# Block-sparse attention into soft MoE: late weight pieces beside the last products, in quarters of rows, and combine turns and identity products in the last chain

## The chip, the cores and the metric

One core of a Trainium2 chip runs the whole program. The metric is the device time of one execution in microseconds, the median of several runs. Five engines work side by side: PE (TensorE, matrix products), DVE (VectorE), ACT (ScalarE), POOL (GpSimd), and SP (SyncE), which here only issues transfers. The transfers run on 16 engines that all queues share.

## The reference, cut to what matters

```python
def _attn_ref(q, k, v, sampled_blocks):          # 4 batches, 8 heads, 768 tokens, head size 64
    scores = scale * np.matmul(q, k.transpose(0, 1, 3, 2))
    # blocks of 32: a query block sees its neighbours, the first and the last block, and three
    # sampled blocks; the first and the last query block see everything
    ...
    attn = softmax(np.where(mask, scores, -1e9))
    return np.matmul(attn, v)

def _moe_ref(x, phi, w1, w2):                    # x: 3072 tokens of 512, phi: 512 x 32 slots
    logits = x @ phi
    d = softmax over the tokens;  slot_input = d.T @ x      # 8 experts, 4 slots each
    slot_out[e] = np.maximum(slot_input[e] @ w1[e], 0.0) @ w2[e]   # 512 -> 1024 -> 512
    c = softmax over the slots;   return c @ slot_out
```

All numbers are float32. [...]

## The kernel before, in words

**Attention.** A unit is two query blocks of one batch, all eight heads. POOL and ACT gather its 256 keys per block into a staging tile `kst` (L414 to L422) and its sampled V blocks into `vrs` (L438). PE makes the scores `s` (L493), DVE the row maximum (L508), ACT the exponential `p` (L513), DVE the turned `ptt` (L520), and PE the products with V, `av` (L571): blocks near the query and the first and last block come straight from the V buffer of the batch (`v0` or `v1`, by turns), sampled ones from `vrs`. DVE divides into `x` (L565 to L567). The first and the last query block are a dense unit (`sd`, `pd`, `ptd`, `avd`).

**First half of the MoE.** Four tiles of `x` make a group. PE turns them (`mxt`, L749), makes logits `ml`, and after an exponential the sums over tokens `ms` (L817). The last group's chain runs from the last `av` over `mxt`, `ml`, `lt`, `mr`, `md`, `ms`, `mc` to `psS` (L996), the slots, and then the first layer can start.

**What sets the order.** `Plan` holds all of this as tasks with a duration for an engine, and a key. `Plan.run` simulates the engines and writes the order out. Weight loads in it are paced: a piece hangs on the PE product that the plan has behind it at 0.22 MB per us.

**The weights** are 64 pieces of 1024 columns x 128 rows (0.5 MB). Two make a first-layer step (`pf`, L1103, pieces 0 to 31) or a second-layer step (`pso`, L1111, pieces 32 to 63). 11 pieces have a place of their own (`wpre`); pieces 11 to 25 go, during the last batch, into buffers that the attention no longer needs: `ktile` (`kw`), `v0`, `ptd`, and the last `ktile`. All these are loaded by quarters: four transfers of 32 rows. Then come nine *places* over the staging tiles (`Place`, 0 to 3 over `kst`, 4 over the scaled q, 5 to 8 over `vrs`), six pieces in `v1`, and after that whatever a step has freed (`done_w`). Of the places, the first five are loaded by quarters, the others, `v1` and all later pieces whole. The transfers of SP's queue use eight semaphores by turns, so that at most eight are under way.

**Second half.** The combine weights `c` of a token are split into two exact parts (`c_head` on DVE, L886, `c_rest` on POOL, L892) and turned by PE (`pc`, L906), one group of four token tiles after the other, between the first steps of the first layer. The output is `po` (L1209), evacuated into `ob` and stored from SP's queue (L1166 to L1174), in two halves of the columns; both halves' stores stand behind all weights in that queue.

```python
    NEND = len(wpool) + (NKST * NP * 256 + NQ * NP * 2 * BLK) // WP
    next_w([Place(n) for n in range(NLB)])
    load_group(LATEW[1])
```

Of the kernel before, what the change touches and what calls it, by code (L numbers as in the profile page):

```python
# [28 lines left out]
D1 = D + 1  # L29
NBZ = NB + 1  # L30
# [21 lines left out]
KW = {"ktile": 3, "v0": 6, "v1": 6, "ptd": 3}  # L52
H1, HALF = 3, 4
# [15 lines left out]
class Plan:  # L69
# [11 lines left out]
    def run(self):  # L81
# [69 lines left out]
        todo = {e: [t for t in order if t.eng == e and t.pre] for e in at}  # L151
        pe = []
# [17 lines left out]
def attn_moe_kernel(ctx, tc, qT, kT, vfull, vtab, sampled, phi, w1, w2, out):  # L170
# [32 lines left out]
    def new_wk(tag):  # L203
        k = KW[tag]
        if tag == "ktile":
            wk[tag] = pk.tile([P, k, WP], F32, name="kw", tag=tag)
        else:
            buf = ptdb if tag == "ptd" else vbuf[int(tag[1])]
            wk[tag] = buf[:, 0:k * WP].rearrange("p (k f) -> p k f", k=k)

    def load_wk(m, tag, j, rows=slice(0, P)):

        return load_w(m + j, None, wk[tag][:, j, :], rows)
# [33 lines left out]
    def index_math():  # L247
# [19 lines left out]
        DVE.tensor_tensor(out=vreg, in0=own, in1=tmp, op=ALU.add)  # L267
# [12 lines left out]
    vrs = [pst.tile([P, 2, NR, 2 * D1], F32, name=f"vrs{n}") for n in range(NVR)]  # L280
# [68 lines left out]
    def warm(t):  # L349

        st = psA.tile([P, 2, 256], F32, tag="s", name="st", bufs=SB)
        for j in range(12):
# [121 lines left out]
    def plan_pair(b, g, n):  # L474
# [21 lines left out]
        t_qk = add(qk, ("PE", 1.1), [t_q] + [k for _, k in kd], n, acq=[("s", s_use[0]), ("s", s_use[1])])  # L496
# [7 lines left out]
        for r in range(2):  # L504
# [18 lines left out]
            t_m = add(top, ("DVE", 0.59), [t_qk], n + 0.1 + 0.01 * r)  # L523
# [55 lines left out]
    def av_heads(T, rs_):  # L579
# [4 lines left out]
        for n, c in enumerate((4, 5)):  # L584
            for r in rs_:
                for g, s_ in G2:
                    av_mm(T.av, 64 * r if one else 0, m, g, r, T.pt[r][s_, c, 0:m // BLK].rearrange("p j q -> p (j q)"),
                          vt[s_, :, (0, NB - 1)[n], r, :], n == 0, False)
        for c in (1, 2):
            for w, u in enumerate(us):  # L590
                for r in rs_:
                    for g, s_ in G2:
                        av_mm(T.av, 64 * r if one else 64 * w, 64, g, r,
                              T.pt[r][s_, c, 2 * w:2 * w + 2].rearrange("p j q -> p (j q)"),
                              vt[s_, :, 2 * u.g + c, r, :], False, False)
        for n in range(NR + 1):
            for w, u in enumerate(us):
                for r in rs_:
                    for j in range(2):
                        i = 2 * u.g + 1 + j  # L600
                        for g, s_ in G2:
                            if n == 0:
# [4 lines left out]
                                v_ = vt[s_, :, k, r, :]  # L607
# [6 lines left out]
    def plan_av(T, n):  # L614
        deps = T.turned + T.staged + [t_v[T.b]]
        use, x_use = [], T.x_use
        if len(T.units) == 1:
# [7 lines left out]
            t_a = add(both, ("PE", 2.5), deps, n + 0.5, acq=[("av", use)])  # L625
            T.out = [add(out, ("DVE", 1.4), [t_a], n + 0.6)]
        else:
# [4 lines left out]
            t_0 = add(lambda t: heads(t, 0), ("PE", 2.2), deps, n + 0.5, acq=[("av", use)])  # L632
            t_a = add(lambda t: heads(t, 1), ("PE", 2.2), [t_0], n + 0.5)
            T.out = [add(lambda t: av_out(T, T.av, 0, P), ("DVE", 1.0), [t_a], n + 0.6, acq=[("x", x_use)])]
        x_use.extend(T.out)
        use.extend(T.out)
        v_use[T.b].append(t_a)
        for u in T.use + list(T.pt_use.values()):
# [5 lines left out]
    def plan_dense(b, j, n):  # L644
# [19 lines left out]
        t_q0, s_acq, s_cost = None, [("s", s_use[0])] * 2 + [("s", s_use[1])] * 2, 1.5  # L664
# [10 lines left out]
        for r in range(2):  # L675
# [24 lines left out]
            t_m = add(top, ("DVE", 0.56 if t_h else 1.12), [t_qk] + t_h, n + 0.1 + 0.01 * r)  # L700
# [7 lines left out]
        if j:  # L708
            use = []

            def dense(t):
                vt = vtile[b]
                T.avd = psA.tile([P, 2, 512], F32, tag="av", name="avd", bufs=1)
                for k in range(NB):
                    for r in range(2):
                        for g, s_ in G2:
                            av_mm(T.avd, 64 - 64 * r, 64, g, r, ptd[r][s_, k].rearrange("p j q -> p (j q)"), vt[s_, :, k, r, :],
# [9 lines left out]
            t_o = add(out, ("DVE", 1.4), [t_a] + T.out, n + 0.6)  # L727
# [14 lines left out]
    def plan_group(gi, Ts, last, final=False):  # L742
        st = Rec()
        t_xT, xT_use = [], []
        for n, T in Ts:
# [10 lines left out]
            t_o = add(out, [("DVE", 0.62), ("ACT", 0.5)], [t_t], n + 2.1, acq=[("xT", x_use)])  # L756
# [76 lines left out]
        t_m = add(top, ("DVE", 0.4), [t_l, state.t_nm], k + 0.1)  # L833
# [65 lines left out]
    def c_turn(g, c4, bank, eng="A"):  # L899
        if g in (3, 4):  # L900
# [4 lines left out]
        for k in range(4):  # L905
            PE.transpose(bank[:, k, :], c4[:, k].rearrange("p r s -> p (r s)"), ident)  # L906
# [40 lines left out]
    for tag, pool, n0, n1 in (("ktile", "k", 3, 5), ("v0", "v", 5, 10), ("ptd", "ptd", 5, 8), ("ktile", "k", 12, 13)):  # L947
        go = lambda j: [qks[min(N - 1, n + n0 + (n1 - n0) * j // KW[tag])]]
        a_w = add(lambda t, tag=tag: new_wk(tag), ("NONE", 0.0), go(0), N + m, acq=[(pool, [t_last])])
        for j in range(KW[tag]):  # L950
            for r in range(0, P, LR):
                add(lambda t, m=m, tag=tag, j=j, r=r: load_wk(m, tag, j, slice(r, r + LR)), ("SP", 0.47), go(j) + [a_w],
                    N + m + j + r / P, byte=4096 * LR, pace=tag != "ktile" or n0 < 12)
# [74 lines left out]
    u[2].append(t_7)  # L1028
    for j, g in enumerate((0, 1, 2, 5)):
        plan_combine(g, N - 4 + j)  # L1030
# [5 lines left out]
    ms.__enter__()  # L1036
    with tc.manual_schedule(engines={E_.SP}):
        plan.run()
# [267 lines left out]
```

## Time and profile before

| | us |
|---|---|
| median of 3 runs | 320.21 (319.62 to 320.77) |
| the profiled execution | 317.94 |
| its span, first to last instruction | 316.2 |
| PE, DVE, POOL, ACT busy | 279.9, 215.0, 180.0, 165.1 |
| moved | 63.62 MB |

In rows of the profile an L and a number is the line of the kernel before, `out<-in` are tiles, and a time is counted from the span's start. "xN" counts instructions; a float32 product stands as two. In rows of stretches, the share is the mean busy share of the 16 transfer engines.

### The profile page before, as it was taken

The page shows a single profiled execution, that of the slowest core. Times are in us where ns is not written, and L with a number is a line of the kernel's source. Part 1 is how long each engine was busy: PE and PEld are TensorE (multiplying, and loading weights), DVE is VectorE, ACT ScalarE, POOL GpSimd, SP SyncE. Part 2 cuts the span into 40 slices and gives each one's busy share as a digit, 9 for nine tenths or more (in the row PEclk, how much of TensorE's full clock was granted, in tenths as well). Part 3 has the DMA queues.
Part 4 walks back from the last instruction along what each step waited for, and adds up shares of the span by engine and source line. Part 5 has one row for each costly group of instructions (what it writes and reads, how often), then busy time and mean ns, then how long its engine had stood idle before and what let it go on. Part 6 is the DMA issues. An engine that isn't in the chain of part 4 may idle for free.

```text
span 316.2 us, 17575 instructions
## 1 busy us (share of the span) xinstructions
PE 279.9 (89%) x7137; PEld 192.1 (61%) x7137; DVE 215.0 (68%) x492; ACT 165.1 (52%) x506; POOL 180.0 (57%) x505
## 2 busy tenths in 40 slices
PE   7489979799999999999989999998997579999950
PEld 7158757457776776677756666866675343356640
DVE  4786867758987799898967898984983256012360
ACT  0838665753666779366777744566750212102450
POOL 2769578765954979594769958568652108000000
PEclk9979999999999999999999999999999958999995
DMA  7926776620256544044754321878977999999998
GB/s 244 401 91 172 208 212 191 171 72 3 63 165 170 175 130 134 3 134 126 195 162 137 82 71 38 221 199 217 230 215 205 224 364 406 412 406 407 383 332 280
DMA packets 32018, 63.62 MB, mean 201 GB/s; under 512 B 5697, under 2 KB 19138, under 8 KB 31938
## 3 DMA queue, kind: packets, MB, share of 16 engines
q1 hardware_dynamic: 31792, 62.37, 63.7%
q8 instruction: 56, 0.92, 1.3%
q14 instruction: 24, 0.20, 0.2%
q10 hardware_dynamic: 146, 0.13, 0.1%
HBM read 56.19 MB, written 6.29 MB: 198 GB/s over the span
## 4 chain that ended last, share of the span: by engine, by line
PE 62%; DMA 9%; DVE 7%; issue 6%; POOL 4%; POOLq 4%; ACT 3%; SPq 1%; ACTq 0%; DVEq 0%
PE av L571 23%; PE s L493 8%; PE avd L571 5%; PE pf L1103 5%; PE pso L1111 5%; DMA q<-in_qT_dram 5%; PE mxt L749 3%; POOLq L319 3%; DMA v<-in_vfull_dram 3%; PE sd L661 3%; PE po L1209 2%; POOL vrs L438 2%; PE ms L817 2%; DMA ktile<-in_kT_dram 2%; DVE x L567 2%
## 5 line engine op out<-in xcount | busy, mean ns | idle before, releaser
L438 POOL COPY vrs<-v 128x260 f32 x264 | 94.8, 404 | 27.4 <-PE av L571 19.1
L513 ACT ACTIVATE p<-s,nm 128x256 f32<-128x256 f32 x176 | 71.3, 477 | 15.5 <-DVE nm L508 14.0
L571 PE MATMUL av<-v,ptt 64*64 64x130 f32 (+2 forms) x1728 | 76.1, 288 | 0.8 <-DMA v<-in_vfull_dram 0.8
L520 DVE STREAM_TRANSPOSE ptt<-p 128x512 f32<-128x512 f32 x88 | 58.1, 691 | 26.5 <-ACT p L513 26.2
L571 PEld LDWEIGHTS av<-v,ptt 64*64 64x64 f32 (+2 forms) x1728 | 50.8, 133 | 25.0 <-issue 16.6
L493 PE MATMUL s<-kst,q 64*32 64x256 f32 x1408 | 50.6, 380 | 6.5 <-POOL kst L422 2.8
L508 DVE TENSOR_REDUCE nm<-s 128x2 f32<-128x512 f32 x88 | 54.7, 677 | 0.4 <-PE s L493 0.2
L414 POOL COPY kst<-ktile 128x384 f32<-128x384 f32 x88 | 42.8, 507 | 13.9 <-PE s L493 13.2
L571 PE MATMUL av<-vrs,ptt 64*32 64x130 f32 x2112 | 47.6, 278 | 2.9 <-issue 2.7
L420 ACT ACTIVATE kst<-ktile 128x128 f32 x171 | 39.0, 302 | 11.0 <-PE s L493 8.1
L493 PEld LDWEIGHTS s<-kst,q 64*32 64x32 f32 x1408 | 30.2, 106 | 18.3 <-issue 4.2
L571 PEld LDWEIGHTS av<-vrs,ptt 64*32 64x32 f32 x2112 | 36.2, 106 | 5.7 <-issue 5.4
L331 ACT COPY xT<-mxt 128x512 f32<-128x512 f32 x23 | 13.4, 582 | 28.4 <-PE mxt L749 28.3
L692 ACT ACTIVATE pd<-sd,nb 128x384 f32<-128x384 f32 x32 | 16.6, 577 | 14.7 <-DVE nb L687 14.1
L422 POOL COPY kst<-ktile 128x128 f32 x93 | 23.2, 293 | 1.8 <-ACT kst L420 0.5
L571 PE MATMUL avd<-v,ptd 64*64 64x130 f32 x768 | 23.4, 271 | 0.8 <-DVE ptd L696 0.4
L571 PEld LDWEIGHTS avd<-v,ptd 64*64 64x64 f32 x768 | 22.0, 132 | 2.8 <-PE s L493 1.7
L457 POOL TENSOR_SCALAR q<-q 128x256 f32<-128x256 f32 x21 | 8.7, 413 | 21.2 <-DMA q<-in_qT_dram 20.8
L749 PE MATMUL mxt<-ident,x 128*128 128x128 f32 x96 | 15.9, 287 | 5.2 <-DVE x L567 5.2
L749 PEld LDWEIGHTS mxt<-ident,x 128*128 128x128 f32 x96 | 10.1, 141 | 17.1 <-DVE x L567 8.0
L455 ACT ACTIVATE q<-q 128x256 f32<-128x256 f32 x27 | 11.2, 417 | 16.8 <-DMA q<-in_qT_dram 16.7
L661 PE MATMUL sd<-ktile,q 64*32 64x384 f32 x256 | 16.7, 492 | 1.8 <-ACT p L513 1.8
(117 smaller groups left out, 279.1 us busy)
## 6 DMA issues: line engine op xcount, KB each, us to landing
w<-in_w_dram SPq DMA_DIRECT2D x64, 128.0 KB, 3.5
w<-in_w_dram SPq DMA_DIRECT2D x15, 512.0 KB, 9.6
v<-in_w_dram SPq DMA_DIRECT2D x12, 512.0 KB, 10.6
q<-in_qT_dram SPq DMA_DIRECT2D x47, 128.0 KB, 2.7
out_dram<-ob SPq DMA_DIRECT2D x22, 256.0 KB, 4.1
ktile<-in_kT_dram SPq DMA_DIRECT2D x48, 96.0 KB, 2.8
kw<-in_w_dram SPq DMA_DIRECT2D x24, 128.0 KB, 3.7
v<-in_w_dram SPq DMA_DIRECT2D x24, 128.0 KB, 3.7
```

What stands on the lines that cost most here:

```text
L414: POOL.tensor_copy(out=st[:, :, w:w + 96], in_=kv[:, :, (i - 1) * BLK:(i + 2) * BLK])
L420: ACT.activation(out=st[:, :, o:o + BLK], in_=src, func=AF.Copy, scale=1.0)
L422: POOL.tensor_copy(out=st[:, :, o:o + BLK], in_=src)
L438: POOL.tensor_copy(out=st[:, :, j:j + 1, :], in_=vf[:, :, ds(t.vals[j], 1), :])
L493: PE.matmul(u.s[r][32 * p:32 * p + 32, j, :], lhsT=u.q[s_, p, j, :], rhs=kd[j][0][s_, p, :], start=True, stop=True)
L508: DVE.tensor_reduce(out=u.nm[r], in_=u.s[r], axis=AX.X, op=ALU.max, negate=True)
L513: ACT.activation(out=u.p[r][:, j, :], in_=u.s[r][:, j, :], func=AF.Exp, bias=u.nm[r][:, j:j + 1], scale=1.0)
L520: DVE.transpose(out=T.pt[r][:, :, 2 * w:2 * w + 2, :].rearrange("p k j q -> p j k q"), in_=u.p[r].rearrange("p j (k q) -> p j k q", k=8))
L571: PE.matmul(av[o:o + m, g, r * 2 * D1:(r + 1) * 2 * D1].rearrange("p (a d) -> p a d", a=2), lhsT=lhsT, rhs=rhs, start=start, stop=stop)
L661: PE.matmul(u.s[r][k][32 * p:32 * p + 32, :], lhsT=T.dq.q[s_, p, j, :], rhs=kt[s_, p, 384 * k:384 * (k + 1)], start=True, stop=True)
L692: ACT.activation(out=u.p[r][k], in_=u.s[r][k], func=AF.Exp, bias=u.nb[r], scale=1.0)
L749: PE.transpose(T.px[:, c, :], T.x[:, c * P:(c + 1) * P], ident)
```

## The change

**Late pieces.** `v1` is no longer one run of six pieces but six slices in an order of their own, and V's blocks stand turned by one in the buffer (`VPOS`: block 0 last), so that the front of both halves of `v1` is not read by the last products. Places and `v1` slices alternate by `LORD`, and the first ten of these pieces are loaded by quarters instead of the first five. The staging tiles `vrs` are allocated in the order in which the last units use them.

**Combine turns.** For groups 0, 1, 2 and 5, the split, the turn and its evacuation are tasks of the plan, keyed into the last chain, with the turn behind the last products.

**Identity products.** Where the plan has PE waiting for more than 0.45 us after the last scores, products of the identity are put in, one per 0.28 us.

**Costs.** The durations of some tasks in the plan differ.

```diff
+VPOS = lambda k: (k - 1) % (NB + 1)
+LORD = [0, 1, 2, 3, 4, 5, -1, -2, -3, -4, 6, 7, 8, -5, -6]
...
+            if t.eng == "PE":
+                if t.start > self.fill[0].fin and t.start - pe_end > 0.45:
+                    self.fill[1](int((t.start - pe_end - 0.15) / 0.28))
+                pe_end = t.fin
...
-            wk[tag] = buf[:, 0:k * WP].rearrange("p (k f) -> p k f", k=k)
+            if tag == LATEW[1]:
+                o = [VH * (j % 2) + WP * (j // 2) for j in range(k)]
+                wk[tag] = [buf[:, c:c + WP] for c in o]
+            else:
+                wk[tag] = buf[:, 0:k * WP].rearrange("p (k f) -> p k f", k=k)
...
-        DVE.tensor_tensor(out=vreg, in0=own, in1=tmp, op=ALU.add)
+        DVE.scalar_tensor_tensor(out=vreg, in0=own, scalar=-1.0, in1=tmp, op0=ALU.add, op1=ALU.add)
...
-    vrs = [pst.tile([P, 2, NR, 2 * D1], F32, name=f"vrs{n}") for n in range(NVR)]
+    vrs = [None] * NVR
+    for n in range(NVR):
+        n = (B * (NB - 2) + n) % NVR
+        vrs[n] = pst.tile([P, 2, NR, 2 * D1], F32, name=f"vrs{n}")
...
-            t_0 = add(lambda t: heads(t, 0), ("PE", 2.2), deps, n + 0.5, acq=[("av", use)])
+            t_0 = add(lambda t: heads(t, 0), ("PE", 2.36), deps, n + 0.5, acq=[("av", use)])
...
-            t_a = add(dense, ("PE", 5.4), T.dturned + [t_v[b]], n + 0.5, acq=[("av", use)])
+            t_a = add(dense, ("PE", 5.75), T.dturned + [t_v[b]], n + 0.5, acq=[("av", use)])
...
+    cb = {}
     for j, g in enumerate((0, 1, 2, 5)):
-        plan_combine(g, N - 4 + j)
+        t_n = plan_combine(g, N - 4 + j)
+        n, p_use, b_use = N + 2 + j, [], []
+        def turn(t, g=g):
+            cb[g] = psA.tile([P, 4, P], F32, tag="s", name="pc", bufs=SB)
+            c_pe(c4[g], cb[g])
+        t_n = add(lambda t, g=g: c_head(g), ("DVE", 0.68), [t_n], n, acq=[("p", p_use)])
+        t_n = add(lambda t, g=g: c_rest(g), ("POOL", 0.95), [t_n], n + 0.1)
+        t_n = add(turn, ("PE", 0.62), [t_n, done[-1][1].t_av], n + 0.2, acq=[("s", b_use)])
+        p_use.append(t_n)
+        b_use.append(add(lambda t, g=g: c_out(g, cb[g]), ("ACT", 0.6), [t_n], n + 0.3, acq=[("ptt", [])] if g in (0, 2) else []))
...
+    plan.fill = max(qks.items())[1], lambda n: warm(None, n)
     with tc.manual_schedule(engines={E_.SP}):
         plan.run()
+    warm(None, 3)
...
+    def load_late(pool, j=None):
+        m = len(wpool)
+        lr = LR if m < MLATE else P
+        for r in range(0, P, lr):
+            if j is None:
+                load_w(m, pool, None, slice(r, r + lr))
+            else:
+                load_wk(m - j, pool.tag, j, slice(r, r + lr))
+        wpool.append(pool)
...
-    NEND = len(wpool) + (NKST * NP * 256 + NQ * NP * 2 * BLK) // WP
-    next_w([Place(n) for n in range(NLB)])
-    load_group(LATEW[1])
+    new_wk(LATEW[1])
+    MLATE = len(wpool) + 10
+    lw, vw = [Place(n) for n in range(NLB)], Group(LATEW[1])
+    for n in LORD:
+        if n < 0:
+            load_late(vw, -1 - n)
+        else:
+            load_late(lw[n])
...
-    for g in (0, 1, 2, 5):
-        c_split(g)
-        g = {1: 0, 2: 1, 3: 2, 4: 5, 6: 3}.get(n)
-        if g is not None:
+        if n == 6:
+            g = 3
             c_turn(g, c4[g], psF.tile([P, 4, P], F32, tag="po", name="pc", bufs=3))
```

How the change moves the instructions shows at two places. The first is SP's queue around the late places (`w_` and a number is one piece in a place; `v_69` is `v1`; a row with 32x1024 is a quarter, with 128x1024 a whole piece). Before:

```order
L197 DMA kw<-in_w_dram 32x1024 x12
L197 DMA w_7056<-in_w_dram 32x1024 x4
L197 DMA w_7061<-in_w_dram 32x1024 x4
L197 DMA w_7066<-in_w_dram 32x1024 x4
L197 DMA w_7071<-in_w_dram 32x1024 x4
L197 DMA w_7076<-in_w_dram 32x1024 x4
L197 DMA w_7081<-in_w_dram 128x1024
L197 DMA w_7083<-in_w_dram 128x1024
L197 DMA w_7085<-in_w_dram 128x1024
L197 DMA w_7087<-in_w_dram 128x1024
L197 DMA v_69<-in_w_dram 128x1024 x6
L197 DMA w_7126<-in_w_dram 128x1024
```

and now, from the third place on:

```order
L207 DMA w_7140<-in_w_dram 32x1024 x4
L207 DMA w_7145<-in_w_dram 32x1024 x4
L207 DMA w_7150<-in_w_dram 32x1024 x4
L207 DMA w_7155<-in_w_dram 32x1024 x4
L207 DMA v_69<-in_w_dram 32x1024 x16
L207 DMA w_7176<-in_w_dram 128x1024
L207 DMA w_7178<-in_w_dram 128x1024
L207 DMA w_7180<-in_w_dram 128x1024
L207 DMA v_69<-in_w_dram 128x1024 x2
L207 DMA w_7195<-in_w_dram 128x1024
```

Place 5 and four slices of `v1` are twenty quarters now, where five whole pieces stood; the stream ahead of them and the pieces from `w_7126` (now `w_7195`) on are in the same order and form.

The second is PE from the end of the last products (`av`) to the first layer (`pf`). Before:

```order
L571 MATMUL av<-vrs_104,ptt 32x130 x2
L749 MATMUL mxt<-ident,x 128x128 x4
L767 MATMUL ml<-xT,phis 32x128 x16
L785 MATMUL lt<-ident,lp 128x128
L961 MATMUL mr<-ident,nmx 1x128
L808 MATMUL md<-ident,dT 128x128
L817 MATMUL ms<-x,d 32x512 x4
L976 MATMUL mc<-ident,row 128x1
L996 MATMUL psS<-selw,sacc 128x32 x4
```

and now (`st` are the identity products, `pc` the combine turns):

```order
L590 MATMUL av<-vrs_106,ptt 32x130 x2
L925 MATMUL pc<-ident,c_6837 128x128 x4
L925 MATMUL pc<-ident,c_6852 128x128 x4
L769 MATMUL mxt<-ident,x 128x128 x4
L925 MATMUL pc<-ident,c_6855 128x128 x4
L925 MATMUL pc<-ident,c_6876 128x128 x4
L787 MATMUL ml<-xT,phis 32x128 x16
L372 MATMUL st<-ident 128x128
L805 MATMUL lt<-ident,lp 128x128
L987 MATMUL mr<-ident,nmx 1x128
L372 MATMUL st<-ident 128x128 x3
L828 MATMUL md<-ident,dT 128x128
```

Two turns stand before `mxt` and two behind it; three, four and three more identity products follow, before `ms`, before `psS` and before the first `pf`, of the 21, one stands ahead of the third `mxt` from the end and six ahead of the second. The first-layer steps follow each other without turns, but for one (group 3, behind the seventh step).

More of the change, by code (lines that the diff above doesn't have):

```diff
@@ L347, in sreg_copy, with warm @@
         DVE.tensor_copy(out=sreg, in_=sraw[0:1, :, :, 0])
-    def warm(t):
+    def warm(t, n=12):
         st = psA.tile([P, 2, 256], F32, tag="s", name="st", bufs=SB)
-        for j in range(12):
+        for j in range(n):
             PE.matmul(st[:, 0, 0:P], lhsT=ident, rhs=ident, start=True, stop=True)
@@ L521, in turn @@
                               in_=u.p[r].rearrange("p j (k q) -> p j k q", k=8))
[L523 removed]
+            t_m = add(top, ("DVE", 0.6), [t_qk], n + 0.1 + 0.01 * r)
             p_use = []
@@ L624, in out @@
                     av_out(T, T.av, 64 * r, 64 * r + 64, slice(r, r + 1), 0)
-            t_a = add(both, ("PE", 2.5), deps, n + 0.5, acq=[("av", use)])
-            T.out = [add(out, ("DVE", 1.4), [t_a], n + 0.6)]
+            t_a = add(both, ("PE", 2.45), deps, n + 0.5, acq=[("av", use)])
+            T.out = [add(out, ("DVE", 1.68), [t_a], n + 0.6)]
         else:
@@ L722, in out @@
                     av_out(T, T.avd, 64 - 64 * r, 128 - 64 * r, slice(r, r + 1), 64)
-            t_a = add(dense, ("PE", 5.4), T.dturned + [t_v[b]], n + 0.5, acq=[("av", use)])
+            t_a = add(dense, ("PE", 5.75), T.dturned + [t_v[b]], n + 0.5, acq=[("av", use)])
             T.ptd_use.append(t_a)
             v_use[b].append(t_a)
-            t_o = add(out, ("DVE", 1.4), [t_a] + T.out, n + 0.6)
+            t_o = add(out, ("DVE", 1.7), [t_a] + T.out, n + 0.6)
             use.append(t_o)
@@ L755, in plan_group @@
             t_t = add(turn, ("PE", 0.6), T.out, n + 2, acq=[("pt", b_use)])
-            t_o = add(out, [("DVE", 0.62), ("ACT", 0.5)], [t_t], n + 2.1, acq=[("xT", x_use)])
+            t_o = add(out, [("DVE", 0.62), ("ACT", 0.48)], [t_t], n + 2.1, acq=[("xT", x_use)])
             T.x_use.append(t_t)
@@ L832, in plan_group @@
         t_p = add(keep, ("ACT", 0.2), [t_l], k + 0.1, acq=[("lp", lp_use)])
-        t_m = add(top, ("DVE", 0.4), [t_l, state.t_nm], k + 0.1)
+        t_m = add(top, ("DVE", 0.5), [t_l, state.t_nm], k + 0.1)
         state.t_nm = t_m
@@ L899, in c_turn, with c_pe, c_out @@
     def c_turn(g, c4, bank, eng="A"):
+        c_pe(c4, bank)
+        c_out(g, bank, eng)
+    def c_pe(c4, bank):
+        for k in range(4):
+            PE.transpose(bank[:, k, :], c4[:, k].rearrange("p r s -> p (r s)"), ident)
+    def c_out(g, bank, eng="A"):
         if g in (3, 4):
@@ L1079, in next_w @@
             elif len(wpool) < NW:
-                for r in range(0, P, LR if len(wpool) < NEND else P):
-                    load_w(len(wpool), pool, None, slice(r, r + (LR if len(wpool) < NEND else P)))
+                load_w(len(wpool), pool)
                 wpool.append(pool)
@@ L1268, in layout @@
     vt = np.zeros((B, NP, BLK, NBZ, 2, D1), v.dtype)
-    vt[:, :, :, :NB, :, :D] = v.reshape(B, 2, NP, NB, BLK, D).transpose(0, 2, 4, 3, 1, 5)
-    vt[:, :, :, :NB, :, D] = 1
+    at = [VPOS(n) for n in range(NB)]
+    vt[:, :, :, at, :, :D] = v.reshape(B, 2, NP, NB, BLK, D).transpose(0, 2, 4, 3, 1, 5)
+    vt[:, :, :, at, :, D] = 1
     a["vtab"] = vt.reshape(B, P, NBZ * 2 * D1)[2:].copy()
```

26 lines of the change are left out of this document (13 added, 13 removed).

## The prediction

> **What bounds the kernel now.** I read the slices of the page first: where is the kernel not at the limit of something?
>
> ```profile
> span 316.2 us, 17575 instructions
> DMA  7926776620256544044754321878977999999998
> GB/s 244 401 91 172 208 212 191 171 72 3 63 165 170 175 130 134 3 134 126 195 162 137 82 71 38 221 199 217 230 215 205 224 364 406 412 406 407 383 332 280
> ```
>
> From the 26th of the 40 slices (198 us) on, the transfers run without a gap; at first at some 200 to 230 GB/s, then at 400. The step is at the 33rd (253 us). Whether the low rate is a choice or a limit shows in the table by stretches (columns: the stretch, its length, busy time of PE, PE's weight loads, VectorE, ScalarE and, where it worked, GpSimd, then PE's granted clock, the busy share of the transfer engines, GB/s).
>
> ```profile
> 242.00:250.00 8.00, 6.03 (x196) 4.40 (x193) 1.06 (x3) 0.81 (x2) 0.33 (x1) 1.00 0.92 226
> 250.00:252.00 2.00, 0.93 (x3) 0.35 (x3) 0.49 (x3) 0.93 (x6) 0.65 (x2) 1.00 1.03 225
> 250.00:255.00 5.00, 2.60 (x14) 1.11 (x14) 2.43 (x9) 1.24 (x7) 0.65 (x2) 0.82 1.01 264
> 255.00:260.00 5.00, 4.35 (x22) 2.79 (x26) 2.51 (x14) 0.62 (x2) 0.00 (x0) 0.50 1.01 374
> 266.00:280.00 14.00, 14.00 (x134) 5.24 (x136) 1.54 (x5) 2.44 (x4) 1.16 (x3) 1.00 1.03 410
> 300.00:310.00 10.00, 4.81 (x28) 3.68 (x27) 5.05 (x10) 4.49 (x10) 0.00 (x0) 0.89 1.04 338
> ```
>
> The share is 0.92 to 1.04 everywhere: the engines are full at 226 GB/s in one stage and full at 410 in another. What differs is the shape, which the issuing queue (SP) shows: start, length, what, how many.
>
> ```profile
> 231.66 7.69 SPq L197 DMA_DIRECT2D kw<-in_w_dram  x12
> 239.46 13.57 SPq L197 DMA_DIRECT2D w<-in_w_dram  x24
> 253.22 4.46 SPq L197 DMA_DIRECT2D v<-in_w_dram  x6
> 286.01 1.73 SPq L197 DMA_DIRECT2D w<-in_w_dram  x2
> w<-in_w_dram SPq DMA_DIRECT2D x64, 128.0 KB, 3.5
> w<-in_w_dram SPq DMA_DIRECT2D x15, 512.0 KB, 9.6
> ```
>
> Up to about 251 us everything is a quarter (32 rows, 128 KB); the 24 issues at 239.46 are the 20 quarters of places 0 to 4 and the four whole pieces (128 rows, 512 KB) of places 5 to 8. From there all weights are whole. The stores, last in this queue, are issued behind the last weight of 287.7 us. So from about 242 us to the end one queue feeds engines that are never free, and **the end is the start of that stream plus the transfer time of what is in it**.
>
> PE's side must be held against this. The chain that ended last (start, length, what):
>
> ```profile
> 241.28 4.80 PE av L571 x163
> 254.93 1.89 PE psS L996 x8
> 257.85 3.64 PE pf L1103 x16
> 261.49 1.05 PE pc L906 x4
> 262.53 1.46 PE pf L1103 x8
> 264.00 0.59 PE pc L906 x4
> 264.58 1.00 PE pf L1103 x8
> 267.75 1.85 PE pf L1103 x16
> 297.52 1.86 PE pso L1111 x32
> 306.35 0.68 DVE ob L1211
> ```
>
> It names PE from 257.85 to the last evacuation at 307.0, but the span ends 9.2 us after that, with stores alone. And PE's last second-layer products end at 299.4, right behind the last weights: those are issued by 287.7, and landing takes about 10 us (9.6 in the row of the 512 KB pieces), so about 298. PE is full as well, but it could not end before that.
>
> **The change part by part.**
>
> *The late places.* In the queue's order before, 20 quarters stand, then 33 whole pieces; after, 40 quarters, then 28 whole pieces. Five whole pieces become twenty quarters. Whole: 0.524 MB at 410 GB/s is 1.28 us; five are 6.4 us. A quarter: 0.131 MB at the 226 GB/s of 242 to 250 us is 0.58 us; twenty are 11.6 us. Difference **+5.2 us** of full engines.
>
> Is 0.58 the transfer or only the issuing? The queue's rows for a part of this stretch:
>
> ```profile
> 241.85 4.14 SPq L197 DMA_DIRECT2D w<-in_w_dram  x9
> L197 SPq DMA_DIRECT2D w<-in_w_dram x18: 311/419/1362, 240.4 to 250.4; - x18
> DMA to landing us min/median/max: 3.0/4.3/4.8
> ```
>
> Nine issues in 4.14 us are 0.46 each, so the queue can issue faster than 0.58; some issues take 1.36. The landing time grows from 3.0 to 4.8 us over the stretch, so a queue builds up behind the transfers, and with quarters alone under way (250 to 252) the share is 1.03 at 225 GB/s. The lower bound is the issuing: 20 x 0.46 = 9.2, difference +2.8. The upper is the slowest two microseconds of the stretch:
>
> ```profile
> 246.00:248.00 2.00, 0.62 (x7) 0.48 (x10) 1.06 (x3) 0.00 (x0) 0.00 (x0) 1.00 0.93 207
> ```
>
> 0.131 MB at 207 GB/s is 0.63; 20 x 0.63 = 12.7, difference +6.3. I take 0.58, since the share says the engines were full.
>
> [...]
>
> *What the places buy.* They are meant to be loaded beside the last products, but the queue doesn't reach place 5 before about 251 us, and the last products end at 246.1 (241.28 + 4.80). Nothing was waiting: between 231.6 and 249.7 the queue shows no wait for any engine. A place that is free earlier is therefore worth 0 here. What stands ahead is the pacing of earlier pieces, and there one wait falls away, since the last paced pieces now hang on products a step earlier:
>
> ```profile
> SPq L197 <- PE av L571: 0.3, 1, 0.3
> SPq L197 <- PE s L493: 1.6, 3, 1.1
> ```
>
> (224 to 231.6 us, and 212 to 224.) I take **-0.3**. If the other wait went too it would be -1.9, but quarters at 217 GB/s already fill most of that time; the other end is 0.
>
> *Combine turns.* Sixteen transposes leave the first layer (1.05 + three at 0.59 = 2.8 us of PE), with eight bit operations on VectorE, eight subtractions on GpSimd and four evacuations on ScalarE. They go beside and behind the last products, to about 236 to 250 us:
>
> ```profile
> 240.00:245.00 5.00, 4.38 (x126) 3.42 (x134) 0.56 (x1) 0.58 (x1) 0.01 (x1) 1.00 0.84 216
> 246.00:258.00 12.00, 6.98 (x63) 4.77 (x67) 4.18 (x17) 2.04 (x8) 0.98 (x2) 0.80 0.99 271
> L892 POOL TENSOR_TENSOR c<-lst,c 128x128 f32<-128x128 f32 x5 | 2.2, 474 | 9.5 <-DVE c L886 9.5
> L886 DVE TENSOR_SCALAR c<-lst 128x128 int32<-128x128 int32 x8 | 2.3, 356 | 0.0
> ```
>
> VectorE and GpSimd are idle from 240 to 245, so most fits. One pair of GpSimd's subtractions (2 x 0.47) now stands ahead of its last six copies of sampled V blocks, and waits there for VectorE: the last products can start up to 1 us later. That delays PE only; the weights wait for it nowhere.
>
> *Identity products.* Twenty-one, at 0.59/4 = 0.15 us each, 3.1 us in the 5.0 us in which PE idles between 246 and 258. They should keep the clock up, which falls to 0.82 and then 0.50 there (table above). Worth for PE: 16 first-layer products in 1.85 us instead of 3.64, eight in 1.00 instead of 1.46, 2.25 us. With the turns, PE is 5.1 us ahead in the first layer. Taken at **0**, because the stream covers it: PE will wait for weights in the second layer instead. If that cover were gone it would be -5.1.
>
> *Costs of tasks, the layout of V, the index arithmetic.* The same instructions; PE's halves of products move past score products in about ten places. PE has 3.8 us idle of 150 between 60 and 210, so little to win or lose there, and 11.7 of 60 at the start:
>
> ```profile
> 0.00:60.00 60.00, 48.32 (x1264) 35.22 (x1264) 41.85 (x97) 35.58 (x111) 41.79 (x123) 0.97 0.68 211
> 60.00:210.00 150.00, 146.23 (x4388) 106.30 (x4389) 126.31 (x276) 95.82 (x301) 109.53 (x310) 1.00 0.44 120
> ```
>
> I take 0, with 1.5 us to either side (an estimate: a part of that idle time). It moves the stream's start with it.
>
> **Sum.** +5.2 - 0.3 = +4.9. The profiled execution took 317.94 us with a span of 316.2; the same kernel's median is 320.21, so 2.3 longer than the profiled one. A span of 321.1, an execution of 322.8 under the profiler, and **325.1 us** as the median.
>
> **The rivals.**
>
> *The quarters cost only their issuing.* For it: 0.46 us in the row of nine. Against it: share 1.03 at 225 GB/s. Then +2.8 - 0.3 = +2.5: 322.7.
>
> *Faster: PE bounds the last stage.* The place is the first layer, where the queue waits for the places that PE frees:
>
> ```profile
> SPq L197 <- PE pf L1103: 5.5, 5, 2.8
> SPq L197 <- DMA w<-in_w_dram: 5.5, 6, 0.9
> ```
>
> (258 to 275 us.) If these 5.5 us held the transfers up, a PE that is 5.1 us ahead would bring all the rest forward, and the slower quarters would pass in time that was waited anyway: 320.2 - 5.1 = 315.1. It decides from the point where the transfer engines run empty in that wait. Against it: 410 GB/s at 1.03 right through (eight transfers are queued, some 10 us of work). [...]
>
> *The attention gets faster.* If better task costs won half of the 11.7 us at the start, 5.9 - 4.9: 319.2. Nothing shows which wait would go.
>
> *No change.* Quarters that cost only their issuing (+2.5), less an attention that is 1.5 us faster and 1 us of the second pacing wait: 320.2.
>
> **How the numbers follow.** Forecast 0.62, with a range of its own of 323.0 to 327.8 (+2.8 at the low end by the bounds; +6.3 and 1.3 of a slower attention at the high one, or a PE that cools while it waits). Issuing alone 0.18. PE bounds 0.09, attention 0.04, no change 0.07. A measurement here tells 0.3% (1 us) from no change: slower 0.80, within 0.07, faster 0.13. The range that leaves 2 in 10 out runs from 320.8 to 327.8: it holds the forecast's and nearly all of the issuing's case.
>
> **What would show it.** Right: 226 GB/s at a full share goes on to about 262 us instead of 251; the last whole weight is issued near 292.5 instead of 287.4; PE starts its first layer earlier, shows no 0.5 clock at 255 to 260, and waits for weights in the second layer, which it doesn't now; the stores shift as a block. Wrong: more than 300 GB/s while quarters alone are under way, or a last weight issued before 288.

## The result and the profile after

The change took **329.32 us** (median of 4 runs, 326.92 to 330.02), the kernel before in the same comparison 319.91 (4 runs, 316.79 to 320.77): a ratio of 1.0311, 95% interval 1.0255 to 1.0367. It is slower, by 9.4 us where the forecast had 4.9, and 1.5 us above the top of the range of 320.8 to 327.8. The profiled execution took 329.86, with a span of 328.0 instead of 316.2. Medians here and below are over all executions of a kernel, ratios over those within 1.5% of its fastest.

I follow the profile of the change in the order of the prediction. The slices of the page first (one is 8.2 us now):

```profile
span 328.0 us, 17681 instructions
PEclk9799989999999999999999999999999999959875
DMA  7935766520366441153655024778767899999998
GB/s 245 398 91 175 197 175 188 153 76 9 101 192 181 129 136 61 43 154 108 177 150 156 21 71 120 205 207 224 218 197 202 211 234 395 408 410 406 373 278 282
```

The low rate lasts to the 33rd slice, 271 us, and the 400 GB/s start behind it; before, the step was at 253. What the queue issued there (start, length, what, how many), and how long its last two weights took to land:

```profile
244.25 15.47 SPq L207 DMA_DIRECT2D w<-in_w_dram  x24
259.82 7.58 SPq L207 DMA_DIRECT2D v<-in_w_dram  x16
297.01 1.59 SPq L207 DMA_DIRECT2D w<-in_w_dram  x2
...
L207 SPq DMA_DIRECT2D w<-in_w_dram x2: 328/328/328, 297.0 to 298.3; - x2
DMA to landing us min/median/max: 10.2/10.2/10.2
```

For the kernel before, the same view of its last two weights:

```profile
L197 SPq DMA_DIRECT2D w<-in_w_dram x2: 327/327/327, 286.0 to 287.4; - x2
DMA to landing us min/median/max: 10.6/10.6/10.7
```

Two delays can be read off. The first late place is issued at 244.25 instead of 239.46: **4.8 us late before a single one of the new quarters has been issued.** From there to the last weight's landing it is 308.5 - 244.25 = 64.2 us instead of 298.1 - 239.46 = 58.6: **5.6 us for the quarters**, where the forecast had 5.2. The span grew by 11.8; the remaining 1.4 lie behind the last weight. The medians are only 9.4 apart, since the profiled execution of the kernel before lies 2.0 below its median and that of the change 0.5 above: some 2.4 of these 11.8 us are spread between executions.

The stretches of the change (columns as in the prediction):

```profile
242.00:250.00 8.00, 7.84 (x248) 6.32 (x232) 2.97 (x10) 0.59 (x1) 5.62 (x14) 1.00 0.72 201
250.00:255.00 5.00, 4.52 (x71) 3.40 (x55) 1.51 (x5) 2.90 (x6) 0.90 (x2) 1.00 0.76 207
255.00:260.00 5.00, 4.76 (x37) 3.52 (x37) 1.99 (x7) 1.20 (x6) 0.09 (x1) 1.00 0.89 199
260.00:265.00 5.00, 4.90 (x46) 2.63 (x49) 3.98 (x18) 0.62 (x2) 1.39 (x2) 1.00 0.86 234
290.00:295.00 5.00, 4.81 (x40) 1.98 (x36) 1.08 (x4) 0.60 (x2) 0.00 (x0) 0.50 1.03 410
```

PE's granted clock is 1.00 where it was 0.82 and 0.50 before. But the transfer engines, with quarters, are busy for 0.72 to 0.89 only, at 199 to 234 GB/s. The prediction had them full, so something else holds the rate here. The trace of the queue shows what: most of the forty issues take 0.42 us and stand 0.05 us apart, and three take 1.40 to 2.49 us. One of the three holds a wait of 1.3 us for the last products, by the profile. Only the last five issues start when an earlier transfer lands. An experiment below comes back to this.

PE's side, by tile (minimum, median and maximum duration in ns, first and last start): first the kernel before, then the change, then the change's waits of PE from 255 us on (total, times, longest).

```profile
L1103 PE MATMUL pf<-w,sT x68: 592/605/1063, 257.8 to 278.6; 128*32 128x512 f32 x68
```

```profile
L1158 PE MATMUL pf<-w,sT x68: 589/592/617, 261.6 to 276.9; 128*32 128x512 f32 x68
```

```profile
PE pso L1166 <- DMA w<-in_w_dram: 3.9, 7, 0.7
PE pso L1166 <- DMA v<-in_w_dram: 1.2, 3, 0.5
PE pso L1166 <- DMA ptd<-in_w_dram: 1.1, 2, 0.6
```

The first layer takes 15.3 us instead of 20.8, so PE gained 5.5 us there (forecast 5.1). It then waits 6.2 us for weights in the second layer, which it did not before.

**Where the 4.8 us come from.** PE's order of scores and products differs from about 35 us on. PE before, between 38 and 48 us (start, length, what, and in brackets the idle time ahead of it and its end):

```profile
40.28 1.71 PE L571 MATMUL av<-v,ptt 64*128 64x130 f32 x40
41.79 0.97 PE L571 MATMUL av<-vrs,ptt 64*32 64x130 f32 x48
44.31 1.46 PE L493 MATMUL s<-kst,q 64*32 64x256 f32 x32 [1.56 <-ACT p L513]
45.70 1.71 PE L571 MATMUL av<-v,ptt 64*128 64x130 f32 x40
```

and in the change, with ACT beside it:

```profile
39.32 0.95 PE L590 MATMUL av<-vrs,ptt 64*32 64x130 f32 x48
40.14 1.22 PE L512 MATMUL s<-kst,q 64*32 64x256 f32 x32
...
42.13 0.62 PE L512 MATMUL s<-kst,q 64*32 64x256 f32 x2
45.63 1.64 PE L512 MATMUL s<-kst,q 64*32 64x256 f32 x30 [2.89 <-ACT p L532]
47.20 2.69 PE L590 MATMUL av<-v,ptt 64*128 64x130 f32 x40
...
39.85 0.84 ACT L532 ACTIVATE p<-s,nm 128x256 f32<-128x256 f32 x2 [1.05 <-DVE nm L527]
44.23 0.42 ACT L474 ACTIVATE q<-q 128x256 f32<-128x256 f32 x1 [3.55 <-DMA q<-in_qT_dram]
44.56 1.02 ACT L532 ACTIVATE p<-s,nm 128x256 f32<-128x256 f32 x2
```

PE starts the second set of scores at 42.13, issues two instructions of it and then waits 2.89 us for a score buffer, which ScalarE's exponential frees. That exponential stands in ScalarE's queue behind the scaling of a q whose transfer lands late: ScalarE stands still for 3.55 us. Over the whole attention (8 to 245 us) this wait of PE is 1.6 us before and 5.6 in the change:

```profile
PE s L493 <- ACT p L513: 1.6, 1, 1.6
```

```profile
PE s L512 <- ACT p L532: 5.6, 4, 2.9
```

These waits don't add up to the 4.8 us by themselves. Counted by PE's instructions in the two traces, the 900th starts 4.9 us later than before, the 2100th (at 80 us) only 2.2 later, and the 6300th (at 235 us) 4.7 later. So more than half of the first delay is caught up, and as much is lost again later: from 60 to 210 us PE is busy for 143.07 us instead of 146.23.

The theory to be tested: the change is two costs that add, the quarters (5.2) and the changed durations, which give PE another order in the attention (3 to 5). The rivals: the 4.8 us are spread between executions, or PE bounds the end.

### The profile page after: what moved, and what is told of

The parts are those of the page before. It is cut to its first block, busy times and chain, and to the rows that moved or that the text cites. A ratio compares the mean times of both kernels' runs of the same rounds, so it can differ in the third digit from the quotient of the medians.

```text
span 328.0 us, 17681 instructions
## 1 busy us (share of the span) xinstructions
PE 289.3 (88%) x7179; PEld 195.3 (60%) x7179; DVE 215.6 (66%) x495; ACT 164.6 (50%) x505; POOL 181.4 (55%) x503
## 4 chain that ended last, share of the span: by engine, by line
PE 44%; DMA 23%; DVE 12%; issue 6%; SPq 4%; ACT 2%; POOLq 2%; POOL 2%; ACTq 2%; DVEq 0%
PE av L590 22%; DMA v<-in_w_dram 8%; DMA q<-in_qT_dram 7%; DMA w<-in_w_dram 6%; PE s L512 6%; PE avd L590 3%; PE sd L681 3%; PE mxt L769 3%; DVE x L586 3%; DVE ptt L539 3%; SPq L207 3%; DMA v<-in_vfull_dram 2%; DVE nm L527 2%; PE po L1262 2%; POOLq L338 2%
## 5 line engine op out<-in xcount | busy, mean ns | idle before, releaser
L457 POOL COPY vrs<-v 128x260 f32 x264 | 96.0, 408 | 31.5 <-PE av L590 23.6
L532 ACT ACTIVATE p<-s,nm 128x256 f32<-128x256 f32 x176 | 72.3, 477 | 15.3 <-DVE nm L527 13.2
L539 DVE STREAM_TRANSPOSE ptt<-p 128x512 f32<-128x512 f32 x88 | 59.0, 694 | 20.3 <-ACT p L532 20.0
L512 PE MATMUL s<-kst,q 64*32 64x256 f32 x1408 | 54.8, 389 | 10.2 <-ACT p L532 5.6
L527 DVE TENSOR_REDUCE nm<-s 128x2 f32<-128x512 f32 x88 | 55.5, 672 | 1.2 <-PE s L512 0.9
L590 PE MATMUL av<-vrs,ptt 64*32 64x130 f32 x2112 | 46.2, 274 | 1.9 <-issue 1.9
L512 PEld LDWEIGHTS s<-kst,q 64*32 64x32 f32 x1408 | 29.5, 107 | 23.6 <-ACT p L532 8.6
L590 PEld LDWEIGHTS av<-vrs,ptt 64*32 64x32 f32 x2112 | 35.5, 105 | 4.1 <-issue 3.7
L350 ACT COPY xT<-mxt 128x512 f32<-128x512 f32 x20 | 11.7, 585 | 24.4 <-PE mxt L769 23.0
L681 PE MATMUL sd<-ktile,q 64*32 64x384 f32 x256 | 17.7, 501 | 1.2 <-ACT p L532 0.8
```

The source lines that it names most:

```text
L457: POOL.tensor_copy(out=st[:, :, j:j + 1, :], in_=vf[:, :, ds(t.vals[j], 1), :])
L512: PE.matmul(u.s[r][32 * p:32 * p + 32, j, :], lhsT=u.q[s_, p, j, :], rhs=kd[j][0][s_, p, :], start=True, stop=True)
L527: DVE.tensor_reduce(out=u.nm[r], in_=u.s[r], axis=AX.X, op=ALU.max, negate=True)
L532: ACT.activation(out=u.p[r][:, j, :], in_=u.s[r][:, j, :], func=AF.Exp, bias=u.nm[r][:, j:j + 1], scale=1.0)
L539: DVE.transpose(out=T.pt[r][:, :, 2 * w:2 * w + 2, :].rearrange("p k j q -> p j k q"), in_=u.p[r].rearrange("p j (k q) -> p j k q", k=8))
L590: PE.matmul(av[o:o + m, g, r * 2 * D1:(r + 1) * 2 * D1].rearrange("p (a d) -> p a d", a=2), lhsT=lhsT, rhs=rhs, start=start, stop=stop)
```

## The experiments

The first five undo a part of the change or do one part alone.

**Durations alone.** The kernel before with the durations of the change in its plan, all thirteen; three of them:

```diff
-            t_0 = add(lambda t: heads(t, 0), ("PE", 2.2), ...
+            t_0 = add(lambda t: heads(t, 0), ("PE", 2.36), ...
-            t_a = add(dense, ("PE", 5.4), ...
+            t_a = add(dense, ("PE", 5.75), ...
-            t_o = add(out, ("DVE", 1.4), [t_a] + T.out, n + 0.6)
+            t_o = add(out, ("DVE", 1.7), [t_a] + T.out, n + 0.6)
```

> The kernel before with the change's task durations alone: the attention in the order of the change, places, turns and identity products as before. Theory A (the new order of the attention costs time of its own: in the two profiles the products stand 4.2 us later from about 50 us on): 3 to 5 us slower than before, so about 323 to 325. Theory B (those 4.2 us are the spread between two executions; the kernel before itself ran from 316.8 to 320.8): within 1 us of before.

Measured: a median of 322.76 (316.85 to 324.39) against 319.43 of the kernel before, but a ratio of 0.9994 (0.9932 to 1.0056), which rests on three of the ten executions. The median speaks for the theory, the ratio for the rival: inconclusive by itself, so no run shows what the durations cost the kernel before.

**The change with the durations of before.**

```diff
-            t_o = add(out, ("DVE", 1.7), [t_a] + T.out, n + 0.6)
+            t_o = add(out, ("DVE", 1.4), [t_a] + T.out, n + 0.6)
```

(and the other twelve likewise)

> The change with the task durations of before: the attention in the old order, the late pieces, turns and identity products as in the change. Theory A: 3 to 5 us faster than the change, so 5 to 7 slower than before, and the first place is issued near 239.5 us again and not at 244.2. Theory B: like the change, 9 to 10 us slower than before.

Measured: 324.98 (323.83 to 327.69), ratio 1.0198 (1.0135 to 1.0261), so 1.1% or 3.6 us below the change. Its queue:

```profile
239.83 13.47 SPq L207 DMA_DIRECT2D w<-in_w_dram  x24
253.63 8.08 SPq L207 DMA_DIRECT2D v<-in_w_dram  x16
292.04 1.65 SPq L207 DMA_DIRECT2D w<-in_w_dram  x2
```

The first late place is back at 239.83; from there to the last weight's landing it is 63.6 us, 5.0 more than before. That is near the 5.2 of the twenty quarters, though it holds a wait of 1.1 us for the last products.

**Five late pieces by quarters, not ten** (the new durations stay):

```diff
-    MLATE = len(wpool) + 10
+    MLATE = len(wpool) + 5
```

> The change, with the first five late pieces by quarters, as before, and not ten. If the transfers of quarters set the end (0.58 us each against 1.28 for a whole piece): 5 to 6 us faster than the change, so about 4 slower than before. If the quarters cost only their issuing: 2 to 3 us faster than the change. If PE's end sets the time: no difference.

Measured: 323.56 (322.81 to 324.56), ratio 1.0118 (1.0076 to 1.0160), 1.9% or 6.2 us below the change.

**All late pieces whole** (the new durations stay):

```diff
-    MLATE = len(wpool) + 10
+    MLATE = len(wpool)
```

> The change, with all late pieces whole. If the transfers of quarters set the end, twice the gain of the kernel with five by quarters, 10 to 12 us faster than the change, so 0 to 2 us faster than before, less what the first places now wait for the products that still read them. If only the issuing counts: 5 us faster than the change. If whole pieces in the last chain slow other work down, the last chain from the end of the products to the first layer is longer than the 11.8 us of before.

Measured: 316.98 (315.63 to 323.7), ratio 0.9949 (0.9911 to 0.9987): another 1.7% or 5.4 us, and faster than the kernel before although the new durations stay.

**Turns, identity products and layout alone**: the durations of before, and five pieces by quarters as before.

> The change with the old durations and five late places by quarters as before: what is left of the change is the combine turns beside the last products, the identity products, the layout of V and the index arithmetic. Theory A (the late stream sets the end, PE's 5 us in the first layer are worth nothing): the time of the kernel before, 319.9, within 1 us; by the sum from the run with forty quarters, 324.98 - 5 x 1.04 = 319.8. Rival (PE bounds the last stage): 315, 5 us faster than before.

Measured: 317.03 against 317.34, ratio 1.0012 (0.9971 to 1.0054), as theory A has it. What PE gains in the first layer is worth nothing measurable while the quarters stand in the stream.

**The same with all late pieces whole.**

> The change with the durations of the kernel before (so PE's order in the attention is the old one) and with all ten late places of w by whole pieces of 128 rows, none by quarters. Theory A (the end is the start of the late stream plus its transfer time; a quarter takes 0.58 us of full transfer engines, four of them 2.32 against 1.28 for the whole): ten places by 1.04 us less than in the run with the old durations and forty quarters (324.98), so 314.6, and 5 us below the kernel before; the two costs add, so it is also 4 to 5 us below... no more than 3 us below the run with all whole and the new durations (316.98), by the attention that is then earlier. Theory B (the new order of the attention costs nothing, the difference was spread): the same as with all whole and the new durations, 317. Theory C (PE bounds once the quarters are gone, since its second layer waits for evacuations): no gain over 317 either, with PE busy without waits for weights up to its last product.

Measured: 312.11 (310.42 to 314.01) against 317.34, ratio **0.9864** (0.9771 to 0.9957), faster than both kernels. Theory A expected 5 us below the kernel before, the ratio gives 4.3; against the run with the new durations (0.9949) it is 2.7. Its stretches:

```profile
255.00:260.00 5.00, 4.74 (x44) 3.32 (x47) 3.42 (x18) 0.62 (x2) 0.00 (x0) 1.00 1.03 412
...
285.00:290.00 5.00, 5.00 (x67) 2.98 (x55) 1.38 (x2) 2.15 (x4) 0.00 (x0) 1.00 1.03 408
```

Transfers and PE are now full together; PE no longer waits for weights.

**The kernel before with all late pieces whole** and nothing else, so without turns and identity products:

```diff
-    NEND = len(wpool) + (NKST * NP * 256 + NQ * NP * 2 * BLK) // WP
+    NEND = len(wpool)
```

> The kernel before with its first five late places by whole pieces too, and nothing else (no combine turns or identity products beside the last chain). Theory A (the late stream sets the end as long as PE keeps up): five places by 1.04 us, 5.2 faster if PE keeps up. But PE's products in the first layer end at 279.2 there, against 274.0 with the turns and the identity products, and the prediction put 5.1 us on that once the cover is gone: so PE would bound, and I expect 1 to 2 us faster only, with PE's last product of the second layer some 298, over 2 us behind the landing of the last weight. Rival (PE's place in the first layer is worth nothing here either): the full 5 us, ratio 0.984, PE's last product within 1 us of the last weight.

Measured: 320.46 against 319.73, ratio 1.0018 (0.9970 to 1.0066). Nothing, less still than the 1 to 2 us that I expected. The profiled execution (322.27) lies above most of this kernel's, so I read only what happens within it: its stretches, and the waits of its queue from 230 to 300 us.

```profile
285.00:290.00 5.00, 5.00 (x80) 3.46 (x84) 0.35 (x2) 0.59 (x1) 0.00 (x0) 1.00 1.02 409
300.00:305.00 5.00, 5.00 (x61) 2.86 (x59) 1.91 (x4) 2.27 (x5) 0.00 (x0) 1.00 0.98 326
```

```profile
SPq L197 <- PE pf L1103: 10.5, 6, 5.1
SPq L197 <- PE av L571: 5.3, 2, 3.9
```

PE is full to the end of the weights: its last products of the second layer start at 303.4, 2.7 us after the last weight has landed (300.7), as the theory has it. The queue, faster now, waits 10.5 us for places that the first layer frees (5.5 before) and 5.3 for places that the last products free. That is the case named in the prediction as the cover that is gone: the same turns, identity products, layout and order of places that are worth 0 beside quarters (ratio 1.0012) are together worth 1.54% or 4.9 us beside whole pieces (0.9864 against 1.0018; a run of the same comparison, below, gives 0.9871). How much of it is PE's place and how much the layout, which frees the places earlier, no run tells apart.

**One duration.** Of the thirteen, one decides in the plan: with the dense evacuation back at 1.4, and the other twelve as in the change, PE's order is that of before up to its 3263rd product.

```diff
-            t_o = add(out, ("DVE", 1.7), [t_a] + T.out, n + 0.6)
+            t_o = add(out, ("DVE", 1.4), [t_a] + T.out, n + 0.6)
```

> The change with one number set back: the duration that the planner takes for the dense avd evacuation, 1.7 to 1.4 (the other twelve changed durations stay). PE's order then is that of the kernel before up to its 3263rd product, where the combine turns stand. Theory A (the new order puts score products ahead of products that are ready, and PE waits 4 us for score buffers that ScalarE frees): as the run with all old durations, 325 (+5.0 to +5.5 against the kernel before in the same job), first late place issued 4 us earlier than in the change (244.25), and PE's waits of the s products on p down from 5.6 to 1.5 us. Rival (the longer time has to do with other durations or with the spread): 328 to 329, the first late place near 244.

Measured: 326.18 against 319.73, ratio 1.0172 (1.0089 to 1.0255), so it does what all thirteen do (1.0198), within that uncertainty. The first late place is issued at 241.57, 2.7 us earlier than in the change, where I had expected 4. PE's waits of its scores between 30 and 60 us:

```profile
PE s L512 <- POOL q L476: 1.3, 1, 1.3
PE s L512 <- POOL vrs L457: 0.6, 1, 0.6
PE s L512 <- ACT p L532: 0.5, 1, 0.5
```

against 4.1 us for the exponential alone in the change:

```profile
PE s L512 <- ACT p L532: 4.1, 2, 2.9
```

The same with all late pieces whole:

> The change with that one number set back, and all ten late places by whole pieces. Theory A: as the run with the old durations and all whole (ratio 0.986, 312.1): 0.98 to 0.99 of the kernel before. Rival (the order isn't it): 0.995, as the run with the new durations and all whole.

Measured: 315.77 against 319.73, ratio 0.9871 (0.9794 to 0.9947), as the run with all durations of before (0.9864) and as theory A has it, though the interval just touches the rival's 0.995.

How much of the 4.8 us at the first late place is the order shows when all traces are put beside each other. With the new order it is issued at 244.25, 243.55, 244.86 and 241.96; with the order of before at 238.73 to 241.57 in seven kernels that issue the same stream ahead of it. But the kernel before with whole pieces, also in the old order, had it at 243.10. So the order moves it by some 3 us, and single executions differ by as much.

**Quarters of columns.** The prediction left open whether a quarter costs its transfer or its issuing. With the durations of before, a quarter becomes 256 of the 1024 columns in all 128 rows; number and size stay.

```diff
-        lr = LR if m < MLATE else P
-        for r in range(0, P, lr):
-            load_w(m, pool, None, slice(r, r + lr))
+        lc = WP // 4 if m < MLATE else WP
+        for c in range(0, WP, lc):
+            load_w(m, pool, None, slice(0, P), slice(c, c + lc))
```

> As the run with the old durations and ten late places by quarters (324.98), but a quarter is 256 of the 1024 columns in all 128 rows, instead of 32 rows with all columns: the same forty transfers of 128 KB. [...] Rival (a transfer of 128 KB is slow whatever its shape, by its fixed cost): the same 325 at about 225 GB/s and a full share. Rival (rows of 1 KB instead of 4 KB are slower for the engines): 325 or slower, with a full share.

Measured: 322.98 against 317.34, ratio 1.0216 (1.0111 to 1.0321): no gain over rows (1.0198). In microseconds it is 2.0 less than with rows, but the kernel before was 2.1 less as well in this comparison. I had estimated up to 4.8 us less than with rows, from forty issues at the 0.46 us of the nine before instead of 0.58: that is wrong. Both rivals have a full share, and are wrong on the engines (0.79 to 0.81). Stretches and issues with quarters of rows:

```profile
250.00:255.00 5.00, 4.45 (x32) 2.92 (x31) 2.42 (x9) 1.20 (x6) 0.63 (x2) 1.00 1.03 239
255.00:260.00 5.00, 4.84 (x44) 2.99 (x48) 3.52 (x16) 0.62 (x2) 0.85 (x1) 1.00 1.02 248
...
L207 SPq DMA_DIRECT2D w<-in_w_dram x24: 310/419/1562, 239.8 to 253.0; - x24
L207 SPq DMA_DIRECT2D v<-in_w_dram x16: 310/313/997, 253.6 to 261.4; - x16
```

and of columns:

```profile
250.00:255.00 5.00, 4.60 (x35) 3.30 (x35) 1.99 (x7) 1.19 (x6) 0.08 (x1) 1.00 0.81 251
255.00:260.00 5.00, 4.89 (x46) 2.63 (x49) 3.99 (x18) 0.62 (x2) 1.39 (x2) 1.00 0.79 254
...
L207 SPq DMA_DIRECT2D w<-in_w_dram x24: 367/430/1669, 238.7 to 251.5; - x24
L207 SPq DMA_DIRECT2D v<-in_w_dram x16: 363/430/1241, 252.0 to 259.9; - x16
```

The share falls from 1.03 to 0.80, so rows do fill the engines in this run and columns don't. But forty issues take from 239.8 to 261.4 with rows and from 238.7 to 259.9 with columns, 21.6 and 21.2 us, or 0.55 and 0.54 from one to the next.

The traces give two reasons for the same number. With columns the issues stand back to back at 0.43 us and 0.04 between them, and three take 1.05 to 1.67: the queue's issuing holds the rate. With rows that is so up to about 250 us. From there on most issues take only 0.31 and begin as the transfer eight before them lands (at most eight are under way): the transfers hold it. Two limits lie on each other here: the transfer of 32 rows (0.131 MB at 226 to 248 GB/s: 0.53 to 0.58 us) and the issuing (0.54). Why single issues take over 1 us isn't settled, and no run had more than eight transfers under way.

Why 32 rows fill the engines at 239 to 248 GB/s, where 128 rows take 0.79 to 0.81 of them at 251 to 254, no run shows. The emptier engines save nothing here, since the issuing is as slow (0.54 us).

**More whole pieces.** As the fastest run, and the second group beside the keys (twelve quarters) by three whole pieces as well.

```diff
-            for r in range(0, P, LR):
+            lr = LR if n0 < 12 else P
+            for r in range(0, P, lr):
```

> As the run with the old durations and ten whole places, and the second group of the three weight pieces beside the keys (twelve quarters, issued at 231.7 us in the profile before) by three whole pieces too. Theory A (each quarter in the stream from 231 us on costs 0.58 us, each whole 1.28): 12 x 0.58 - 3 x 1.28 = 3.1 us earlier than that run, 311 to 312, if the places are free by then. Theory C (PE bounds): no more than 1 us earlier; then the last weight lands earlier and PE's last product doesn't follow it within 1 us.

Measured: 316.41 (313.08 to 319.33) against 317.34, ratio 0.9951 (0.9901 to 1.0001): not faster than without it (0.9864, 0.9771 to 0.9957), if not slower, a miss of theory A. Theory C, no more than 1 us earlier, fits the time, but the earlier last weight that it names didn't come: it lands at 297.0 instead of 293.5. The profiled execution took 317.78, a little above its median. Its stretches, and its queue's waits from 230 to 270 us:

```profile
240.00:245.00 5.00, 2.10 (x17) 1.80 (x16) 2.05 (x8) 0.00 (x0) 2.10 (x6) 1.00 1.02 404
260.00:265.00 5.00, 4.90 (x46) 2.43 (x49) 4.31 (x20) 0.62 (x2) 1.75 (x2) 1.00 0.30 70
...
SPq L207 <- PE pf L1159: 11.8, 4, 10.3
SPq L207 <- PE av L590: 10.6, 3, 4.9
```

Theory A had a condition, "if the places are free by then", and they are not: the queue comes to them earlier and waits 10.6 us for the last products, where it waited 0.3 without this edit. Then the engines run empty (0.30), since the queue waits 10.3 us at a stretch for the first layer, which starts at 261.3 instead of 258.2. Part of that delay is a stop of PE: it stands still for 2.9 us in the middle of the last products, waiting for nothing that the profile shows, while whole pieces fill the engines at 404 GB/s. Why it stood still isn't settled, nor whether other executions have this stop.

**Together.** Ratios to the kernel before, by late pieces loaded by quarters ("turns etc." are the turns, the identity products, the layout and the order of places):

| | none | five | ten |
|---|---|---|---|
| kernel before | 1.0018 | 1 | not run |
| turns etc., durations of before | 0.9864 | 1.0012 | 1.0198 |
| the same, one duration of before | 0.9871 | not run | 1.0172 |
| turns etc., durations of the change | 0.9949 | 1.0118 | 1.0311 |

Each measured entry is uncertain by 0.4 to 0.9%, and the comparisons were not all made together, but the steps agree. In the kernels with turns, five more pieces by quarters cost 1.5, 1.9, 1.7 and 1.9% (4.7 to 6.2 us); in the kernel before, where PE is full to the end without them, nothing. The durations cost 0.9, 1.1 and 1.1% against those of before (2.7 to 3.6 us), and by the one duration 0.8 and 1.4%. Some of these single steps lie within their uncertainty; it is the five together that show the cost. With durations of before the plan also puts in 19 identity products instead of 21.

## Why the prediction was wrong, step by step

**The quarters, +5.2: the size is right, the reason half of it.** 5.6 in the traces (1.3 of it a wait for the last products), 4.7 to 6.2 in four pairs of runs with turns. I took 0.58 because the engines were full. In the change itself they are not (0.72 to 0.89) and the issuing holds the rate; with quarters of columns they aren't either (0.79 to 0.81), and the time stays. The lower bound of 0.46 for the issuing came from nine issues without a long one among them; over forty it is 0.54, which gives 20 x 0.54 - 6.4 = +4.4 and not +2.8. The rival "only their issuing" and the forecast were nearly one case, and that they were is luck.

**The pacing, -0.3:** lost in the attention's delay; no run tells it apart.

**Places that are free earlier, 0: right beside quarters.** Beside whole pieces the wait shows: 5.3 us for the last products in the kernel before with whole pieces, 0.3 us in the run with turns and layout. What it is worth there by itself no run shows.

**Combine turns and identity products, 0, and -5.1 if the cover is gone.** The 0 is right, with ratio 1.0012: PE's 5.5 us became waits for weights, as forecast. For the -5.1 the runs give -4.9 us, but with the layout and the order of places in it, so the near agreement may be luck, and what PE's place alone is worth there stays open. The granted clock was 1.00 from 250 to 260 us in the change and in five other runs with turns and identity products, and 0.82 and 0.50 before; no run has the identity products alone. The top of the range also named a PE that cools while it waits: in the change the clock was 0.84 and 0.50 from 285 to 295 us, where PE was busy for 2.77 and 4.81 of each 5, and no run shows what that cost.

**Costs of tasks, 0 with 1.5 us to either side: this step failed.** By five comparisons of runs they make the kernel 2.5 to 4.4 us slower, where the range held 1.3 for them. I argued from averages: PE idles 3.8 us of 150 between 60 and 210 us and 11.7 of the first 60, "so little to win or lose there". But idle time bounds only what an order can win. What it can lose lies in the waits that it makes new, and those weren't in the profile of before except as a hint, the one wait of 1.6 us of scores for an exponential. I had seen PE's halves of products move past score products, and did not ask what the moved scores need: a buffer that ScalarE frees, behind a q that waits for its transfer.

That the durations do it is shown by the runs with other durations, and down to one number of them, which alone puts the attention's order back. That the score buffers are the way in which they do is only read from the traces: 5.6 us of that wait in the change, 6.3, 6.7 and 4.9 in the three other runs with the new order, 0.5 to 1.9 in all with the order of before. It is not the whole way, since half of the first delay is caught up by 80 us, and the run with 4.9 us of that wait has its first late place only 2.5 us after the kernel before. No run had more score buffers, so how the delay reaches the end stays open.

**The signs named:** the low rate past 262 us (it went to about 271), the last whole weight late (298.3 against the 292.5 forecast), no 0.50 clock at 255 to 260, and waits for weights in the second layer all came. The full share did not (0.72 to 0.89). "PE starts its first layer earlier" did not: it starts at 261.6, 3.8 us later than before, since the last products end 4.2 later. The remaining 1.4 us of the span lie behind the last weight. From its landing to the last store's it takes 17.0 us before and 18.4 after, but 16.7 to 18.8 in the eleven experiments, so this is within the spread.

Sum as it came, by the ratios: about 6 for the quarters and 3.5 for the durations, 9.4. With the durations of before the change takes 324.98, and the forecast was 325.1.

## What to carry to other kernels

A task's duration in a planner is an edit of the program's order: compare the orders, and for each place where they differ ask what the moved instruction takes (a buffer, a load) and who must free it, instead of bounding the effect by the idle time that there is. Two improvements that cover each other each measure as nothing (whole pieces alone 1.0018; turns, identity products and layout alone 1.0012) and together give 1.4%: an edit whose gain ends up in a new wait should be tried with that wait taken away too. And a transfer split into four was held by its issuing here (0.54 to 0.55 us from one to the next) as much as by its shape (0.53 to 0.58 us for 32 rows): pieces of 128 KB came to 239 to 254 GB/s from one queue, with 32 rows as with 128, where whole pieces came to 357 to 412 in the fastest run.

## What the runs showed of the hardware

- Forty transfers of 128 KB from one queue went out 0.54 to 0.55 us apart, in 128 rows as in 32. With 128 rows the issuing held them (0.43 us each, three of 1.05 to 1.67). With 32 rows, from about the middle on, most waited for the landing of the one eight before. The rate was 239 to 254 GB/s, at a busy share of the engines of 1.02 to 1.03 with 32 rows and of 0.79 to 0.81 with 128 rows. In the change, also with 32 rows, the issuing held them for longer, at 199 to 234 GB/s and a share of 0.72 to 0.89.
- With whole pieces of 512 KB under way at 404 GB/s beside the last products, PE stood still for 2.9 us with no releaser in the profile. This was seen in one profiled execution, and its cause is open.
- Transfers and PE are full side by side from 255 to 290 us in the fastest run (PE 4.74 to 5.00 us of each 5, shares of 0.99 to 1.03, 357 to 412 GB/s), and neither the faster stream alone (1.0018) nor the faster PE with the new layout alone (1.0012) shows.
